# One-row matmul replaced by a ScalarE add, and a 64-row product widened to 128 rows, in an attention and two-MLP kernel

## The chip, the cores and the metric

The kernel runs on one core of a Trainium2 chip. The metric is the device time of one launch in microseconds. Three runs of the kernel before took 1377.99, 1380.79 and 1382.39 us, so the median is 1380.79 us. Five engines work side by side, each through its own queue in order: PE (TensorE), DVE (VectorE), ACT (ScalarE), POOL (GpSimd) and SP, which issues the DMAs.

## The reference

Attention over 4 batches, 8 heads, 576 positions and 64 channels, in which each row keeps only its 32 largest scores, then two MLPs (512 to 2048 to 512) over the 2304 tokens.

```
scores = scale * q @ k.T
kth    = 32nd largest of each row
p      = exp(where(scores >= kth, scores, -1e9) - max)
x      = p / (sum(p) + 1e-9) @ v
x      = softplus-like(x @ w_in) @ w_out           # first MLP
h      = x @ w_in2;  out = (h - tanh(h)) @ w_out2  # second MLP
```

The change is in the third and fourth lines: the product of p and v, and the 1e-9 in the divisor.

## The kernel before, in words

Every float32 operand is split into two float16 halves (high and low), and a product is made of three: high by high, high by low and low by high.

A tile is 128 queries of one head (kind "n", 128 tiles), or 64 left-over queries of each of two heads (kind "l", 16 tiles); there are 144. Its steps lie on all engines. `front` makes the scores on PE (L554), and ACT copies them out of PSUM (L557). `chain` finds the 32nd largest on DVE, with four MAX8 and three MATCH_REPLACE8 over 576 columns (L566, L569). `exps` and `mask` make p on ACT (L134). `turn` casts p to its halves (ACT L596, POOL L597 and L598) and transposes them by DMA into `pT`, of two buffers. `back` multiplies `pT` by the values and normalizes. Its result goes by another DMA transpose into x, the first MLP's input.

In `back`, a head's product is a run of matmuls of 65 columns: 64 channels and a column of ones in `vh`, which gives the sum of p. The 576 keys are four blocks of 128 and one of 64 (SL). For a full block t there are L612, L613 and L614. In the last block, partitions 0 to 63 of `pT[:, NB]` hold the high half of p, and 64 to 127 its low half; the values of that block stand twice in `vh` and `vl`, on both halves of the partitions. L615 is over all 128 rows: high by high and low by high at once. L616 is high p by low v, over 64 rows. L618 multiplies a row of ones (1 partition, float32) by eps and adds it into the sum's column; a float32 matmul shows as two records. DVE then takes the reciprocal straight from PSUM (L629), POOL multiplies it by a factor for kind "l" alone (L631), ACT scales the 64 channels out of PSUM (L636). A tile of kind "n" has one such run of matmuls ("side"), one of kind "l" two: 160 in all.

PSUM has four buffers "tp", which `back` (px), the MLPs' first product (h) and small column sums (pn) share.

An MLP step is 24 matmuls of 256 columns (h: L680 to L682), an activation (ACT L134, L701, POOL L702, L705, for the second MLP also DVE L699), and, three or four steps later, 24 matmuls of 256 columns (L723 to L725) or 12 of 512 (L731 to L733). The program emits steps for about one tile's worth of tokens with each tile as soon as the weights of that MLP have been split. The splitting (L277 to L316, all engines) fills the early part. A scheduler then orders each engine's queue by priorities and its own estimates.

Of the kernel before, what the change touches and what calls it, by code (L numbers as in the profile page):

```python
# [13 lines left out]
AF = mybir.ActivationFunctionType  # L14
# [59 lines left out]
def topk_attention_two_mlps(  # L74
# [17 lines left out]
    nc = tc.nc  # L92
    P = 128
    B, H, S, D = q.shape
# [3 lines left out]
    NB = 4  # L98
    SL = S - NB * P
# [45 lines left out]
    def tiny(n=1):  # L145
        o = used_[0]
        used_[0] += n
        return tiles_[:, o : o + n]

    ones = tiny()  # L150
# [3 lines left out]
    eps = tiny()  # L154
    nc.gpsimd.memset(eps, 1e-9)
    eps2 = tiny()
# [4 lines left out]
    def nm(s):  # L161
        uid[0] += 1
        return f"{s}_{uid[0]}"
# [438 lines left out]
    def back(st):  # L602
        vi, it = st.vi, st.it
        ps = ps_t.tile([P, 512], F32, tag="tp", name=nm("px"))
        if st.kind == "n":
            sides = [(ps[:, 0 : D + 1], st.h, 0, P)]
        else:
            sides = [(ps[0:SL, j * (D + 1) : (j + 1) * (D + 1)], j, j * SL, (j + 1) * SL) for j in range(2)]
        for o, h, c0, c1 in sides:
            vh, vl = vi.vhl[:, 0, h], vi.vhl[:, 1, h]  # L610
            for t in range(NB):
                nc.tensor.matmul(o, st.pT[:, t, c0:c1], vh[:, t, 0 : D + 1], start=(t == 0), stop=False)  # L612
                nc.tensor.matmul(o, st.pT[:, t, c0:c1], vl[:, t, 0 : D + 1], start=False, stop=False)  # L613
                nc.tensor.matmul(o, st.pT[:, NB + 1 + t, c0:c1], vh[:, t, 0 : D + 1], start=False, stop=False)  # L614
            nc.tensor.matmul(o, st.pT[:, NB, c0:c1], vh[:, NB, 0 : D + 1], start=False, stop=False)  # L615
            nc.tensor.matmul(o, st.pT[0:SL, NB, c0:c1], vl[0:SL, NB, 0 : D + 1], start=False, stop=False)  # L616

            nc.tensor.matmul(o[:, D : D + 1], ones[0:1].to_broadcast([1, c1 - c0]), (eps2 if st.soft else eps)[0:1], start=False, stop=True)  # L618
        if st is it.sts[0]:
            it.x = ap.tile([P, 2, P], F16, tag="xs", bufs=NXS, name=nm("xs"))  # L620
            if XE:
                it.x32 = ap.tile([P, P], F32, tag="x32", bufs=NXS, name=nm("x32"))
        rows = P if st.kind == "n" else SL
        ns = len(sides)
        r = sp.tile([P, 2], F32, tag="r2", bufs=3, name=nm("r2"))

        pv = ps[0:rows, 0 : ns * (D + 1)].rearrange("p (j d) -> p j d", j=ns)
        rr = r[0:rows, 0:ns].unsqueeze(2)
        nc.vector.reciprocal(rr, pv[:, :, D : D + 1])  # L629
        if st.kind == "l":  # L630
            nc.gpsimd.tensor_mul(r[0:rows, 0:ns], r[0:rows, 0:ns], fl[vi.b][0:rows].to_broadcast([rows, ns]))  # L631
        for i, (o, h, c0, c1) in enumerate(sides):
            c = slice(h * D, (h + 1) * D)
            sc, src = r[0:rows, i : i + 1], o[:, 0:D]
            if XE:
                nc.scalar.activation(it.x32[0:rows, c], src, AF.Copy, scale=sc)  # L636
            else:
                nc.scalar.activation(it.x[0:rows, 0, c], src, AF.Copy, scale=sc)
                nc.vector.scalar_tensor_tensor(it.x[0:rows, 1, c], src, sc, it.x[0:rows, 0, c], op0=ALU.mult, op1=ALU.subtract)
        if st is not it.sts[-1]:  # L640
            return
        if XE:
            if XE == 1:
                nc.scalar.copy(it.x[0:rows, 0, :], it.x32[0:rows])
            else:
                nc.vector.tensor_copy(it.x[0:rows, 0, :], it.x32[0:rows])
            nc.gpsimd.tensor_sub(it.x[0:rows, 1, :], it.x32[0:rows], it.x[0:rows, 0, :])
        nc.sync.dma_start_transpose(
            out=it.chunk.x.block(vi.p)[:, :, it.col : it.col + rows],
            in_=it.x[0:rows].rearrange("p r c -> p (r c)"),  # L650
        )
# [203 lines left out]
    for ch, ts, _ in plan:  # L855
        for p in range(NP):
# [9 lines left out]
            for h in range(2):  # L866
                for ti, it in enumerate(its):
                    st = ST()
# [3 lines left out]
                if h == 0 and lc is not None:  # L872
                    it = ST()
                    it.spec, it.chunk, it.col, it.sts = vspec, lc, (ch.b % 2) * SL, []
                    st = ST()
# [71 lines left out]
    c1 = [0]  # L947
# [65 lines left out]
    for n in range(-1, NT + 2 + BL):  # L1013
# [12 lines left out]
        if last is not None:  # L1026
            ch = last.it.chunk
            if not hasattr(ch, "x"):
                while ch.T // P > len(xy_free):
                    force_step(n - 2 - BL)  # L1030
                ch.x = new_xy(ch.T, "x")
            with tc.high_priority(HP):
                back(last)
        if n + 1 < NT and n + 1 >= 0:
            st = tiles[n + 1]
# [74 lines left out]
```

## Time and profile before

| | us |
|---|---|
| median of three runs | 1380.79 |
| the profiled execution | 1381.37 |
| its span, first to last instruction | 1379.6 |
| PE busy | 1137.5 (82%) |
| DVE busy | 994.6 (72%) |
| ACT busy | 951.4 (69%) |
| POOL busy | 841.0 (61%) |

The busy shares are means over stages that differ. Up to about 414 us PE is busy half of the time or less, while the weights are split; from there to 1242 us tiles and MLP steps run together; after 1242 us only MLP steps are left. The stages have to be read one by one. The profiled execution is 1.8 us longer than its span.

### The profile page before, as it was taken

How to read it: one execution, taken by the hardware profiler on the slowest of the kernel's cores; microseconds unless marked ns; L12 is line 12 of the kernel's file. 1: busy time of each engine (PE TensorE's matmuls, PEld its weight loads, DVE VectorE, ACT ScalarE, POOL GpSimd, SP SyncE). 2: the span in 40 equal slices, each digit the busy share in tenths (PEclk: the TensorE clock that was granted, in tenths of full speed). 3: DMA queues.
4: the chain of work that ended last, by engine and by line, in shares of the span. 5: the costliest groups of instructions: out<-in, count | busy, mean ns of one | idle time of the engine just before them, and what ended most of it. 6: DMA issues, size and time to landing. Idle time of an engine off the chain costs nothing.

```text
span 1379.6 us, 28066 instructions
## 1 busy us (share of the span) xinstructions
PE 1137.5 (82%) x10098; PEld 882.1 (64%) x10098; DVE 994.6 (72%) x2150; ACT 951.4 (69%) x1786; POOL 841.0 (61%) x1194
## 2 busy tenths in 40 slices
PE   2232437975479999998999999999999899999998
PEld 1131225864358766767667987687767677896875
DVE  5998879979997697865878679759977688611011
ACT  7987988889886787655666767667764667643332
POOL 2679867887874665644666556557764366543342
PEclk9999998985568999989899999999999799999999
DMA  8956786565666458334456335435543254110000
GB/s 263 277 169 176 205 225 165 110 138 132 159 150 167 102 120 153 64 83 95 91 107 129 74 68 94 90 93 119 119 95 75 45 101 92 28 26 1 17 9 16
DMA packets 322524, 153.18 MB, mean 111 GB/s; under 512 B 270160, under 2 KB 302416, under 8 KB 322384
## 3 DMA queue, kind: packets, MB, share of 16 engines
q1 hardware_dynamic: 322384, 151.39, 47.8%
q8 instruction: 79, 1.29, 0.4%
q14 instruction: 61, 0.50, 0.1%
HBM read 73.04 MB, written 15.37 MB: 64 GB/s over the span
## 4 chain that ended last, share of the span: by engine, by line
PE 55%; DMA 11%; POOL 10%; DVE 9%; ACT 8%; issue 7%; SPq 1%; POOLq 0%; ACTq 0%
PE h L680 8%; PE h L681 8%; PE h L682 8%; DMA pT<-hl 4%; PE y L733 4%; PE y L731 4%; PE y L732 4%; PE s L554 3%; PE y L723 3%; PE y L724 3%; PE y L725 3%; DVE m L566 3%; DVE x L569 2%; PE px L618 2%; POOL wlo L316 2%
## 5 line engine op out<-in xcount | busy, mean ns | idle before, releaser
L566 DVE MAX8 m<-x 128x8 f32<-128x576 f32 x432 | 318.9, 749 | 3.5
L702 POOL TENSOR_SCALAR r<-r,gs 128x512 f32<-128x512 f32 (+1 forms) x160 | 109.1, 682 | 200.3 <-ACT g L701 175.6
L597 POOL TENSOR_TENSOR hl<-x,hl 128x512 f16<-128x512 f32 x144 | 170.4, 1183 | 90.6 <-ACT hl L596 76.7
L569 DVE MATCH_REPLACE8 x<-m,x 128x576 f32<-128x576 f32 x288 | 213.2, 741 | 0.0
L554 PE MATMUL s<-kT,qT 128*128 128x288 f16 x512 | 118.8, 324 | 82.6 <-ACT ssb L557 48.4
L705 POOL TENSOR_TENSOR g<-r,g 128x512 f16<-128x512 f32 (+1 forms) x160 | 172.4, 1078 | 9.4
L134 ACT ACTIVATE r<-h,hin 128x512 f32<-128x512 f32 (+1 forms) x160 | 102.1, 639 | 110.1 <-PE h L682 93.9
L680 PE MATMUL h<-y,whi 128*128 128x256 f16 (+1 forms) x640 | 166.0, 269 | 8.5 <-ACT y L751 8.5
L699 DVE SCALAR_TENSOR_TENSOR r<-h,hin,r 128x512 f32<-128x512 f32 (+1 forms) x80 | 55.1, 690 | 159.5 <-ACT r L134 153.1
L680 PE MATMUL h<-x,whi 128*128 128x256 f16 (+1 forms) x640 | 167.7, 270 | 0.7 <-DMA x<-xs 0.7
L682 PE MATMUL h<-x,wlo 128*128 128x256 f16 (+1 forms) x640 | 167.5, 270 | 0.0
L681 PE MATMUL h<-x,whi 128*128 128x256 f16 (+1 forms) x640 | 167.5, 270 | 0.0
L724 PE MATMUL y<-g,whi 128*128 128x256 f16 (+1 forms) x640 | 164.5, 267 | 2.1 <-POOL g L705 2.1
L681 PE MATMUL h<-y,whi 128*128 128x256 f16 (+1 forms) x640 | 166.0, 268 | 0.0
L682 PE MATMUL h<-y,wlo 128*128 128x256 f16 (+1 forms) x640 | 165.5, 268 | 0.0
L723 PE MATMUL y<-g,whi 128*128 128x256 f16 (+1 forms) x640 | 163.9, 268 | 1.0 <-ACT g L701 0.5
L725 PE MATMUL y<-g,wlo 128*128 128x256 f16 (+1 forms) x640 | 164.4, 267 | 0.0
L701 ACT ACTIVATE g<-r,gs 128x512 f16<-128x512 f32 (+1 forms) x160 | 107.6, 674 | 73.6 <-PE y L724 36.5
L566 DVE MAX8 m<-ssb 128x8 f32<-128x576 f32 x144 | 107.9, 749 | 60.3 <-ACT ssb L557 60.0
L612 PE MATMUL px<-vhl,pT 128*128 128x65 f16 (+1 forms) x640 | 97.5, 209 | 63.0 <-DMA pT<-hl 60.7
L680 PEld LDWEIGHTS <-whi 128*128 128x128 f16 x1280 | 128.2, 100 | 21.6
L681 PEld LDWEIGHTS <-whi 128*128 128x128 f16 x1280 | 127.9, 100 | 19.9 <-issue 1.0
(141 smaller groups left out, 3246.6 us busy)
## 6 DMA issues: line engine op xcount, KB each, us to landing
whi<-in_moe_w_in_dram SPq DMA_DIRECT2D x8, 1024.0 KB, 5.6
wlo<-in_moe_w_in_dram SPq DMA_DIRECT2D x6, 1024.0 KB, 7.5
wlo<-in_moe_w_out_dram SPq DMA_DIRECT2D x6, 1024.0 KB, 5.1
vd<-vhl SPq DMA_DIRECT2D x16, 330.0 KB, 3.2
vhl<-vd SPq DMA_DIRECT2D x16, 330.0 KB, 3.5
kd<-kT SPq DMA_DIRECT2D x32, 160.0 KB, 2.0
whi<-in_moe_w_out_dram SPq DMA_DIRECT2D x5, 1024.0 KB, 4.9
kT<-kd SPq DMA_DIRECT2D x32, 160.0 KB, 2.5
```

The lines of the kernel that those rows point to most:

```text
L554: nc.tensor.matmul(ps[:, hf, 0:HS], lhs, rhs[:, hf * HS : (hf + 1) * HS], start=(i == 0), stop=(i == len(prods) - 1))
L566: return lambda: nc.vector.max(m[:, 8 * i : 8 * i + 8], src)
L569: return lambda: nc.vector.match_replace(x, m[:, 8 * i : 8 * i + 8], src, NEG)
L597: nc.gpsimd.tensor_sub(hl[:, S + SL : 2 * S], st.p[:, 0 : NB * P], hl[:, 0 : NB * P])
L680: nc.tensor.matmul(o, hi[:, f], xhi, start=(d == 0), stop=False)
L681: nc.tensor.matmul(o, hi[:, f], xlo, start=False, stop=False)
L682: nc.tensor.matmul(o, lo[:, f], xhi, start=False, stop=(d == ND - 1))
L702: nc.gpsimd.tensor_scalar(r, r, gs, 1.0, op0=ALU.mult, op1=ALU.mult)
L705: nc.gpsimd.tensor_sub(glo, r, ghi)
L723: nc.tensor.matmul(o, hi[:, dd], gh, start=first, stop=False)
L724: nc.tensor.matmul(o, hi[:, dd], gl, start=False, stop=False)
L725: nc.tensor.matmul(o, lo[:, dd], gh, start=False, stop=fin)
```

## The change

L616 and L618 go. L617 takes L616's place, over all 128 rows: the upper 64 rows add the low half of p by the low half of v, a term that was left out so far. ACT adds eps to the sum on its way from PSUM to the small tile r (L628), with eps as a bias of one number per partition, and DVE takes the reciprocal of r in place (L629).

```
-            nc.tensor.matmul(o, st.pT[0:SL, NB, c0:c1], vl[0:SL, NB, 0 : D + 1], start=False, stop=False)
-
-            nc.tensor.matmul(o[:, D : D + 1], ones[0:1].to_broadcast([1, c1 - c0]), (eps2 if st.soft else eps)[0:1], start=False, stop=True)
+
+            nc.tensor.matmul(o, st.pT[:, NB, c0:c1], vl[:, NB, 0 : D + 1], start=False, stop=True)
...
-        nc.vector.reciprocal(rr, pv[:, :, D : D + 1])
+        nc.scalar.activation(rr, pv[:, :, D : D + 1], AF.Identity, bias=(eps2 if st.soft else eps)[0:rows])
+        nc.vector.reciprocal(r[0:rows, 0:ns], r[0:rows, 0:ns])
```

PE loses 160 instructions of L618 and swaps 160 pairs of load and matmul of L616 for L617's; ACT gains 144 instructions; DVE, POOL and SP keep their counts. The scheduler makes the queues anew. The three places below belong to one tile, whose product runs at about 702 us in the trace of before. PE, the end of the tile's product (px is its PSUM buffer, h that of an MLP step), before and then after:

```order
L614 MATMUL px_8291<-vhl_7703,pT_8174 128x65
L615 LDWEIGHTS pT_8174
L615 MATMUL px_8291<-vhl_7703,pT_8174 128x65
L616 LDWEIGHTS pT_8174
L616 MATMUL px_8291<-vhl_7703,pT_8174 128x65
L618 MATMUL px_8291<-tiny 128x1
L681 LDWEIGHTS whi_93
L681 MATMUL h_8227<-y_7488,whi_93 128x256
```

```order
L614 MATMUL px_8283<-vhl_7695,pT_8166 128x65
L615 LDWEIGHTS pT_8166
L615 MATMUL px_8283<-vhl_7695,pT_8166 128x65
L617 LDWEIGHTS pT_8166
L617 MATMUL px_8283<-vhl_7695,pT_8166 128x65
L681 LDWEIGHTS whi_93
L681 MATMUL h_8219<-y_7481,whi_93 128x256
```

The product ends with L617, and the MLP's L681 follows it as it followed L618; nothing else moved here.

ACT at the same tile (khl and vhl are halves of a later tile's keys and values, g an MLP step's), before and then after:

```order
L557 COPY ssb_8318<-s_8313 128x576
L701 ACTIVATE g_8138<-r_8137,gs_7507 128x512
L477 ACTIVATE khl_8617<-kraw_8094,tiny 128x5x64
L532 ACTIVATE vhl_8511<-v_7694,tiny 128x10x64
L636 ACTIVATE x_1441_8083<-px_8291,r_1481_8307 128x64
```

```order
L557 COPY ssb_8310<-s_8305 128x576
L477 ACTIVATE khl_8609<-kraw_8086,tiny 128x5x64
L701 ACTIVATE g_8130<-r_8129,gs_7500 128x512
L628 ACTIVATE r_1481_8298<-px_8283,tiny 128x1
L532 ACTIVATE vhl_8503<-v_7686,tiny 128x10x64
L636 ACTIVATE x_1441_8074<-px_8283,r_1481_8298 128x64
```

L628 stands behind L477 and L701, whose order has changed, and one instruction ahead of L636.

DVE at the same tile (m and x are those of a later tile's chain), before and then after:

```order
L566 MAX m_8373<-ssb_8318 128x8
L566 MAX m_8281<-x_8282 128x8
L569 MATCH_REPLACE x_8374<-m_8373,ssb_8318 128x576
L629 RECIPROCAL r_1481_8307<-px_8291 128x1
L566 MAX m_8373<-x_8374 128x8
L533 SCALAR_TENSOR_TENSOR vhl_8511<-v_7694,tiny,vhl_8511 128x10x64
```

```order
L569 MATCH_REPLACE x_8366<-m_8365,ssb_8310 128x576
L566 MAX m_8273<-x_8274 128x8
L629 RECIPROCAL r_1481_8298<-r_1481_8298 128x1
L566 MAX m_8365<-x_8366 128x8
L533 SCALAR_TENSOR_TENSOR vhl_8503<-v_7686,tiny,vhl_8503 128x10x64
```

The reciprocal has kept its place between the same steps of the chain, but it now reads what ACT wrote.

## Rows read from the trace of the kernel before

**Rows 1.** Busy us (instructions) by engine, clock, DMA, in three stretches.

```profile
0.00:414.00 414.00, 205.72 (x1566) 163.42 (x1567) 357.77 (x794) 351.27 (x675) 309.05 (x393) 0.86 0.69 181
414.00:1242.00 828.00, 799.18 (x7451) 621.00 (x7450) 622.04 (x1331) 555.56 (x1042) 483.22 (x741) 0.95 0.45 93
1242.00:1380.00 138.00, 132.60 (x1085) 97.71 (x1082) 14.76 (x27) 44.54 (x70) 48.77 (x61) 0.99 0.03 11
```

**Rows 2.** The chain that ended last, 414 to 1242 us, by line.

```profile
by line: PE h L681 10.2%; PE h L680 10.2%; PE h L682 10.0%; PE s L554 5.2%; PE y L733 4.4%; PE y L731 4.3%; PE y L732 4.3%; PE y L723 4.3%; PE y L724 4.2%; PE y L725 4.2%; issue 3.8%; PE px L618 3.3%; DMA pT<-hl 3.0%; PE px L612 2.2%; DMA v
```

**Rows 3.** PE in order of time: start us, us, instruction; a product's end.

```profile
702.20 0.19 PE L614 MATMUL px<-vhl,pT 128*128 128x65 f16 x1
702.22 0.20 PE L615 MATMUL px<-vhl,pT 128*128 128x65 f16 x1
702.35 0.20 PE L616 MATMUL px<-vhl,pT 64*128 64x65 f16 x1
702.48 0.38 PE L618 MATMUL px<-tiny 1*128 1x1 f32 x2
702.79 0.28 PE L681 MATMUL h<-y,whi 128*128 128x256 f16 x1
702.91 0.27 PE L682 MATMUL h<-y,wlo 128*128 128x256 f16 x1
```

**Rows 4.** PE in order of time, an end interleaved with an MLP step.

```profile
619.96 0.19 PE L615 MATMUL px<-vhl,pT 128*128 128x65 f16 x1
619.99 0.27 PE L681 MATMUL h<-x,whi 128*128 128x256 f16 x1
620.19 0.20 PE L616 MATMUL px<-vhl,pT 64*128 64x65 f16 x1
620.33 0.28 PE L682 MATMUL h<-x,wlo 128*128 128x256 f16 x1
620.54 0.38 PE L618 MATMUL px<-tiny 1*128 1x1 f32 x2
620.85 0.28 PE L680 MATMUL h<-x,whi 128*128 128x256 f16 x1
```

**Rows 5.** L618 alone in the first two stretches: PE busy (records), load busy, clock, DMA.

```profile
0.00:414.00 414.00, 22.12 (x88) 18.38 (x88) 0.86 0.69 181
414.00:1242.00 828.00, 42.77 (x232) 32.88 (x232) 0.95 0.45 93
```

**Rows 6.** L629 alone in the same stretches: DVE busy (instructions).

```profile
0.00:414.00 414.00, 6.27 (x40) 0.86 0.69 181
414.00:1242.00 828.00, 16.30 (x104) 0.95 0.45 93
```

**Rows 7.** Groups by line and shape: busy us, mean ns, idle before.

```profile
L636 ACT ACTIVATE x<-px,r 128x64 f32<-128x64 f32 x128 | 39.4, 308 | 42.2 <-DVE r L629 40.7 <-DVE tiny L180 1.4
L343 ACT ACTIVATION_READ_ACCUMULATOR vst<-vst 128x1 f32 x60 | 11.3, 189 | 0.0
L510 ACT ACTIVATE ql<-ql,tiny 128x64 f32<-128x64 f32 x16 | 5.5, 344 | 4.8 <-DMA ql<-in_q_dram 3.8 <-POOL hl L598 0.8 <-DVE tiny L179 0.2
```

**Rows 8.** Waits, 0 to 414 us: us in total, times, longest.

```profile
PE px L612 <- DMA pT<-hl: 54.7, 20, 13.0
PE pn L169 <- ACT wlo L288: 51.1, 19, 8.0
PE s L554 <- ACT ssb L557: 43.5, 19, 7.8
```

**Rows 9.** Waits, 414 to 1242 us.

```profile
DVE r L629 <- PE px L618: 46.0, 27, 6.7
ACT x L636 <- DVE r L629: 36.4, 26, 3.7
PE h L680 <- ACT y L751: 8.5, 2, 4.4
```

**Rows 10.** ACT and DVE in order of time, near 707 us.

```profile
707.31 0.56 ACT L477 ACTIVATE khl<-kraw,tiny 128x320 f16<-128x320 f32 x1 [2.29 <-DMA kT<-khl]
706.90 0.16 DVE L629 RECIPROCAL r<-px 128x1 f32<-128x1 f32 x1
```

**Rows 11.** Busy by engine and clock, two slices around the change of stage.

```profile
345.00:414.00 69.00, 41.33 (x316) 31.96 (x317) 65.55 (x158) 57.23 (x126) 55.56 (x95) 0.60 0.65 154
414.00:483.00 69.00, 64.75 (x606) 55.35 (x605) 49.94 (x124) 49.14 (x103) 37.66 (x56) 0.94 0.59 135
```

## The prediction

> **What bounds the kernel now.** I read the busy time by stretch first, since the change touches PE and ACT and the page's means mix three stages. The reader is to see three kernels in one [rows 1]. Up to 414 us PE works 205.7 us of 414, while DVE (357.8) and ACT (351.3) are both at 85 to 86%: no engine is full, and work passes from one to the next. From 414 to 1242 us PE is busy 799 of 828 us, 97%, at a granted clock of 0.95, with DVE at 75% and ACT at 67%: PE bounds this stage. After 1242 us PE is alone at 96%, and no product of p and v is left there, as L618 has no record [rows 5].
>
> A busy PE may still hide slack, so I read the chain of waits of the middle stage next [rows 2]. Its largest shares are PE's: the listed lines of h, y, s and px add up to 67%. L618 alone, a matmul of one column, holds 3.3% of it. Then I read PE in order of time at the end of a product, for the spacing of starts, since ends are modelled and overlap [rows 3, 4]. Then the waits, for who would be late if PE were early [rows 8, 9].
>
> **PE: what goes.** In the plain form [rows 3] L615 starts at 702.22 and the next step's L681 at 702.79: the end of the product holds PE for 0.57 us. Without L616 and L618 it holds L615 and L617, two 128-row matmuls of 65 columns. Such a one hands over after 0.03 us (L615 to L681) [rows 4], so 0.06 us stay and 0.51 go. In the interleaved form [rows 4] L615 to L680 takes 0.89 us and holds two matmuls of h, worth 0.12 each by the spacing in rows 3; 0.65 are the product's, 0.06 stay, 0.59 go. Where the time goes shows in the same rows: 0.13 us pass before L616 starts where 0.03 is usual, 0.13 more before L618, and 0.31 from L618 to the next matmul.
>
> The Trainium skill ("TensorEngine Tiling (Array Packing)", Key Properties) says that changing the tiling mode drains TensorE. By that rule the 0.13 us ahead of L616 belong to its 64 rows and fall to 0.03 with L617. Without it, they may belong to the end of the product and stay. The rows agree with the rule at one place each, but show no 128-row matmul in L616's position.
>
> How many: the middle stage has 232 records of L618, two each, so 116 sides [rows 5]. At 0.51 to 0.59 us this is 59 to 68 us of PE. I take 0.53, near the plain form, which is the commoner in the stretches I read: 62 us.
>
> How much of that arrives: L618 lies in the chain with 3.3% of 828 us = 27 us [rows 2]. All its 116 sides would be 116 x 0.31 = 36 us. So about 0.76 of them stand where time is made; the others stand where the chain runs over a transpose, DVE or ACT. 62 x 0.76 = 47 us. The ends are 0 (PE only waits longer) and the full 68.
>
> In the first stage 44 sides go as well, at 0.5 us or more each, 22 us of PE or more. PE is half idle there and waits for transposes, for ACT's sums and for its evictions of scores, 149 us in the three longest of its waits [rows 8]. I count this gain as nothing; the idle time covers it. If it did arrive, it would be up to 22.
>
> **ACT: what comes.** 144 instructions L628 of 128x1, from PSUM, with a bias per partition. The trace has none. From below: 189 ns, a read of 128x1 without operands (L343) [rows 7]. From above: 344 ns, 64 columns with a per-partition operand (L510) [rows 7]; L636, from PSUM with 64 columns, takes 308. I take 250, between the ends, since one column is left of 64: 36 us in all, 27 to 50 by the ends.
>
> The 104 tiles of the middle stage [rows 6] bring 26 us, which lift ACT from 556 of 828 to 582 of about 781 us, 75%: hidden beside PE, which runs three to four MLP steps ahead of the activations it waits for. If this cover fails, all 26 are paid. The 40 tiles of the first stage bring 10 us on an engine at 85% in a stage without a full engine. I charge half, 5 us; the ends are a gain of 5 (a shorter PE part in the same chain) and a loss of 25, below.
>
> **DVE: what moves.** The reciprocals stay 144 and read one column of SBUF in place of PSUM. I cost this at nothing: the row of before is 16.30 us for 104, 157 ns each [rows 6], and cannot fall by more. What matters is the wait. DVE waited 46 us for PE at L629 in the middle stage [rows 9], and ACT then 36 us for DVE at L636. Now ACT waits for PE, DVE for ACT, and ACT again for DVE. PE's part comes 0.5 us earlier, L628 and its handover cost about 0.3, so the reciprocal is ready at about the same time if ACT is there. If ACT is not, DVE's next MAX8 stands behind the reciprocal, as the order shows. The scheduler left five or fewer instructions of ACT between L628 and L636 at 112 of 144 tiles, fourteen at most.
>
> Nothing else moves: the number of DMAs and their queue are the same, and by the order the MLP steps stand at the same tiles as before, within a few matmuls. The longer hold of a PSUM buffer px (one more hop, under 1 us) meets four buffers, and no wait of PE for one of them is among the long ones.
>
> **The sum.** 1381.4 (profiled) - 47 + 5 = 1339. The median of the runs lies 0.6 us lower than the profiled execution, inside the rounding: I forecast **1339 us**, with a range of its own of 1318 to 1360 (a share of 0.95 or 0.45 of the 62 us arriving, with the 5 of the first stage).
>
> **Rivals.**
>
> *DVE gets stuck behind ACT (slower).* At 707 us ACT waits 2.29 us for a transpose at L477 until 707.31, then works 0.56 us; DVE's reciprocal starts at 706.90 [rows 10]. In the new order L628 is behind this L477: it would end at about 708.1, and DVE would wait 1.2 us where it waited for nothing. If that is the usual case, the first stage has 40 x 1.2 = 48 us of new waits on an engine with 56 us to spare; charge 40. In the middle stage 104 x 1.2 = 125 us bring DVE from 622 to 747 of 781 us, and half of PE's 47 us is lost. 1381 + 40 - 23 = 1398. It decides once the mean new wait is over 1 us a tile. Against it: DVE already waited for px at 27 of 104 tiles in the middle stage, and the order puts other work between.
>
> *The spacing stays.* If the 0.13 us ahead of the last two matmuls belong to the product's end, 0.57 falls to 0.13 + 0.13 only, and 0.31 a side goes: 116 x 0.31 x 0.76 = 27 us; 1381 - 27 + 5 = 1359.
>
> *Hidden.* PE finishes earlier and waits longer for what the others bring, one for one: 1381, within 4. For it speaks that a third of the chain is not PE's; against it that all of PE's waits for another engine in the middle stage are short, the longest in total 8.5 us [rows 9].
>
> *The clock.* From 345 to 414 us the granted clock is 0.60, the 1.2 GHz level most of the time, with PE busy 41 of 69 us; in the next slice it is 0.94 with 65 [rows 11]. If a sparser PE stayed low for one slice more, that slice's 64.75 us of work would take 64.75 x 0.94 / 0.60 = 101, 37 more: 1376. The Trainium skill ("TensorE: Matmul & The Clock Gate", HAM oscillation) states that pauses between bursts of matmuls throw the clock back to half. The trace agrees in that the low slice is the one with pauses. Against this rival: little PE work leaves one slice, about 3 us of 65.
>
> *All of it.* The full 68 us arrive, and the first stage loses nothing: 1313.
>
> **Chances.** Forecast 0.60; spacing stays 0.08; clock 0.04; all of it 0.10; hidden 0.07; DVE behind ACT 0.11. A change under 0.3% (4 us) can't be told from none here. Faster: 0.60 + 0.08 + 0.04 + 0.10 = 0.82, with the clock's case just on its edge; same 0.07; slower 0.11. The range leaves out the last two and goes down to the full gain less a little for the first stage: 1308 to 1376.
>
> **What would show it.** Right: no spacing over 0.05 us inside the product's end, L617 to the next matmul too; PE's busy share after 414 us near 97% still, in a stage shorter by some 45 us; attention's end at about 1200 in place of 1242 us, the tail after it unchanged; the first 40 tiles done within 5 us of 414; L628 at 0.25 us. Wrong: DVE's wait at L629 for ACT over 100 us in all, or PE's waits in the middle stage grown by 30 us or more, or a spacing of 0.13 us ahead of L617.

## The result and the profile after

The changed kernel takes 1329.05 us (median of 4 runs, 1323.64 to 1331.66) where the kernel before took 1381.59 beside it: a ratio of 0.962, 95% interval 0.958 to 0.965. Forecast were 1339 us, in a range of 1308 to 1376. The profiled execution took 1329.11 us with a span of 1327.1.

The view of busy time by engine in the kernel after, in the three stretches of [rows 1] with the middle one cut where attention now ends; the columns are those of [rows 1]:

```profile
0.00:414.00 414.00, 178.44 (x1457) 141.42 (x1458) 356.95 (x780) 353.03 (x707) 298.48 (x383) 0.82 0.69 180
414.00:1190.00 776.00, 729.32 (x7242) 571.90 (x7241) 624.44 (x1345) 572.18 (x1155) 487.23 (x752) 0.97 0.49 100
1190.00:1327.10 137.10, 132.47 (x1083) 97.61 (x1081) 14.62 (x27) 44.56 (x70) 48.74 (x61) 0.99 0.03 11
```

PE is at 94% in the middle stage, where it was at 97%; DVE rose from 75 to 80%, ACT from 67 to 74%. The last stretch is as it was. To see which stage gave the time, both traces are cut where a tile number is the same: at the 41st reciprocal and at the last one (the 144th). Before:

```profile
0.00:420.50 420.50, 212.22 (x1628) 169.05 (x1629) 364.03 (x807) 356.11 (x687) 313.55 (x398) 0.86 0.69 180
420.50:1220.20 799.70, 770.88 (x7138) 596.13 (x7136) 611.47 (x1309) 541.68 (x1014) 470.84 (x723) 0.95 0.46 95
1220.20:1379.60 159.40, 154.40 (x1336) 116.94 (x1334) 19.07 (x36) 53.57 (x85) 56.64 (x73) 0.99 0.03 10
```

After:

```profile
0.00:431.30 431.30, 192.66 (x1606) 154.02 (x1606) 374.22 (x821) 367.75 (x740) 311.75 (x403) 0.83 0.68 178
431.30:1168.60 737.30, 693.70 (x6851) 540.48 (x6849) 602.71 (x1294) 548.54 (x1105) 466.17 (x718) 0.97 0.50 101
1168.60:1327.10 158.50, 153.87 (x1328) 116.42 (x1325) 19.08 (x36) 53.48 (x85) 56.53 (x73) 0.99 0.03 10
```

The first stage became 10.8 us longer, the middle one 62.4 us shorter, the last 0.9 shorter: 52.5 in all. In the middle PE's busy time fell by 77 us and its idle time rose from 28.8 to 43.6. The granted clock rose there from 0.95 to 0.97. Length times granted clock is the length that the stage would have at 2.4 GHz: 799.7 x 0.95 = 760 and 737.3 x 0.97 = 715, 45 us less. The other 17 us are then what the 1.2 GHz level cost before and no longer costs: the stage spends some 35 us less at that level, at half the clock. (The clock has two digits, so each product is good to some 4 us, and the reckoning takes the whole stage to run at PE's pace.) By the same reckoning PE's busy time fell by 59 us: 770.88 x 0.95 = 732, 693.70 x 0.97 = 673.

PE in order of time at the end of a product, the answer to [rows 3]:

```profile
655.14 0.19 PE L614 MATMUL px<-vhl,pT 128*128 128x65 f16 x1
655.17 0.19 PE L615 MATMUL px<-vhl,pT 128*128 128x65 f16 x1
655.21 0.19 PE L617 MATMUL px<-vhl,pT 128*128 128x65 f16 x1
655.23 0.27 PE L680 MATMUL h<-y,whi 128*128 128x256 f16 x1
```

From L615 to the MLP's next matmul there are 0.06 us, where there were 0.57. The chain of waits from 414 to 1190 us, by line, the answer to [rows 2]:

```profile
by line: PE h L681 7.0%; PE h L680 7.0%; PE h L682 7.0%; DMA pT<-hl 6.8%; issue 6.7%; DVE m L566 4.6%; DVE x L569 4.2%; PE y L724 3.7%; PE y L723 3.7%; PE y L725 3.6%; PE s L554 3.4%; POOL hl L597 2.5%; PE y L731 2.5%; PE y L732 2.4%; PE y 
```

PE's shares are smaller, and the transpose of p, DVE's MAX8 and MATCH_REPLACE8 stand among them now: the next bounds are near. The small instructions by line and shape (busy us, mean ns, idle before), and the waits from 414 to 1190 us, the answer to [rows 7, 9]:

```profile
L628 ACT ACTIVATE r<-px,tiny 128x1 f32<-128x1 f32 x128 | 32.9, 259 | 20.2 <-PE px L617 19.6
L629 DVE RECIPROCAL r<-r 128x1 f32<-128x1 f32 x128 | 18.9, 149 | 14.1 <-ACT r L628 13.8
```

```profile
DVE r L629 <- ACT r L628: 26.4, 15, 5.4
ACT x L636 <- DVE r L629: 22.7, 23, 2.6
ACT r L628 <- PE px L617: 21.3, 20, 2.5
PE px L612 <- DMA pT<-hl: 20.9, 20, 2.1
PE h L680 <- ACT y L751: 9.8, 2, 5.4
```

L628 takes 259 ns. DVE's wait at the reciprocal has fallen from 46.0 us, for PE (38.1 of them up to 1190 us), to 26.4, for ACT; PE waits 20.9 us for the transposes of p, where it waited 5.8 in the same stretch before. In the first stage PE's same three waits grew from 149 us [rows 8] to 182:

```profile
PE pn L169 <- ACT wlo L288: 72.3, 18, 12.5
PE s L554 <- ACT ssb L557: 57.9, 22, 8.8
PE px L612 <- DMA pT<-hl: 52.3, 16, 9.7
```

The granted clock of the first stage can't be read from the column in these views. The view of the kernel after by stretch, for L612 alone (PE busy, load busy, clock, DMA):

```profile
0.00:188.00 188.00, 7.94 (x44) 6.41 (x44) 1.00 0.80 227
192.00:232.00 40.00, 4.39 (x24) 3.02 (x24) 0.50 0.63 149
407.00:440.00 33.00, 1.98 (x16) 1.57 (x16) 1.00 0.65 160
```

The view by source of the same line in the same stretches gives the time of one of its matmuls, all of one shape (ns: least, median, most):

```profile
L612 PE MATMUL px<-vhl,pT x44: 215/243/262, 62.3 to 186.2; 128*128 128x65 f16 x44
L612 PE MATMUL px<-vhl,pT x24: 233/243/247, 194.7 to 227.8; 128*128 128x65 f16 x24
L612 PE MATMUL px<-vhl,pT x16: 190/194/204, 411.5 to 432.1; 128*128 128x65 f16 x16
```

Up to 188 us the column shows 1.00, but the matmul takes the 243 ns that it takes at 0.50, and not 194. In the kernel before it takes 243 ns up to 207 us as well, with 1.00 in the column. So the clock is compared in the middle stage alone.

### The profile page after: what moved, and what is told of

Its sections match the earlier page's. It is cut to its first block, busy times and chain, and to the rows that moved or that the text cites. A ratio compares the mean times of both kernels' runs of the same rounds, so it can differ in the third digit from the quotient of the medians.

```text
span 1327.1 us, 27583 instructions
## 1 busy us (share of the span) xinstructions
PE 1040.2 (78%) x9778; PEld 810.9 (61%) x9778; DVE 996.0 (75%) x2150; ACT 969.8 (73%) x1930; POOL 834.4 (63%) x1194
## 4 chain that ended last, share of the span: by engine, by line
PE 40%; DVE 15%; DMA 13%; POOL 12%; ACT 10%; issue 9%; SPq 1%; POOLq 0%; ACTq 0%; DVEq 0%
PE h L680 6%; PE h L681 6%; PE h L682 6%; DVE m L566 5%; DMA pT<-hl 5%; DVE x L569 5%; PE y L724 3%; PE y L723 3%; PE y L731 3%; PE y L725 3%; PE y L732 3%; PE y L733 3%; POOL hl L597 3%; PE s L554 2%; POOL wlo L316 2%
## 5 line engine op out<-in xcount | busy, mean ns | idle before, releaser
L680 PE MATMUL h<-y,whi 128*128 128x256 f16 (+1 forms) x640 | 162.7, 263 | 10.2 <-ACT y L751 9.8
L681 PE MATMUL h<-x,whi 128*128 128x256 f16 (+1 forms) x640 | 166.7, 269 | 0.0
L681 PE MATMUL h<-y,whi 128*128 128x256 f16 (+1 forms) x640 | 162.4, 263 | 0.0
L682 PE MATMUL h<-y,wlo 128*128 128x256 f16 (+1 forms) x640 | 162.3, 263 | 0.0
L612 PE MATMUL px<-vhl,pT 128*128 128x65 f16 (+1 forms) x640 | 96.3, 209 | 79.6 <-DMA pT<-hl 73.3
L701 ACT ACTIVATE g<-r,gs 128x512 f16<-128x512 f32 (+1 forms) x160 | 107.8, 676 | 57.0 <-PE y L724 25.0
L681 PEld LDWEIGHTS <-whi 128*128 128x128 f16 x1280 | 126.6, 99 | 22.5 <-issue 4.3
```

The source lines that it names most:

```text
L680: nc.tensor.matmul(o, hi[:, f], xhi, start=(d == 0), stop=False)
L681: nc.tensor.matmul(o, hi[:, f], xlo, start=False, stop=False)
L682: nc.tensor.matmul(o, lo[:, f], xhi, start=False, stop=(d == ND - 1))
```

## The experiments

The theory was that PE's time at the end of each product is the price ("PE"). The rivals were that the hop over ScalarE matters, for or against, and that the gain is in how the scheduler's queues fall. All times are medians, beside runs of the kernel before on the same chip (1377.01 in the first group, 1378.55 and 1378.54 in the others); the ratio stands behind, with its 95% interval. The changed kernel's 1329.05 was taken beside 1381.59, so a difference between it and a form below is good to a few us.

**The wide product alone**

```
-  nc.tensor.matmul(o, st.pT[0:SL, NB, c0:c1], vl[0:SL, NB, 0 : D + 1], start=False, stop=False)
+  nc.tensor.matmul(o, st.pT[:, NB, c0:c1], vl[:, NB, 0 : D + 1], start=False, stop=False)
```

> The wide product alone (L617 over 128 rows); the one-row matmul for 1e-9 stays. Theory PE (the end of each product holds PE, and the spacing ahead of a matmul of other rows is the price): only the 0.10 us ahead of the 64-row matmul goes, the one-row matmul still has 0.13 ahead of it and 0.31 behind, so 116 x 0.10 = 12 us of PE go and 9 to 12 arrive: 1370 to 1373 us. Theory 'spacing belongs to the product's end': nothing goes, 1381. Theory 'new order' (the gain is in how the queues fall, not in PE's time): anything, up to the whole 52 us, 1329.

Measured: 1367.67 us, 0.993 (0.990 to 0.996). The scheduler gave every engine the same queue as in the kernel before, so nothing but PE's spacing differs. PE in order of time:

```profile
697.89 0.19 PE L615 MATMUL px<-vhl,pT 128*128 128x65 f16 x1
697.92 0.19 PE L616 MATMUL px<-vhl,pT 128*128 128x65 f16 x1
698.05 0.38 PE L618 MATMUL px<-tiny 1*128 1x1 f32 x2
698.36 0.28 PE L681 MATMUL h<-y,whi 128*128 128x256 f16 x1
```

The 0.13 us ahead of the last product are 0.03 now, those ahead of the one-row matmul have stayed. 116 x 0.10 = 12 us of PE went and 9 arrived, as expected of theory PE. "Spacing belongs to the product's end" is out. What differs in the spacing shows in the weight loads (PEld), in the kernel before and then here:

```profile
702.20 0.10 PEld L615 LDWEIGHTS <-pT 128*128 128x128 f16 x1
702.35 0.09 PEld L616 LDWEIGHTS <-pT 64*128 64x128 f16 x1
```

```profile
697.86 0.10 PEld L615 LDWEIGHTS <-pT 128*128 128x128 f16 x1
697.89 0.10 PEld L616 LDWEIGHTS <-pT 128*128 128x128 f16 x1
```

Over 128 rows the load of L616 starts with the matmul before it (697.89), 0.03 us ahead of its own; over 64 rows it starts only with its own matmul, 0.13 us behind L615's start.

**The add on ScalarE alone** (the changed kernel with the last product over 64 rows)

```
-  nc.tensor.matmul(o, st.pT[:, NB, c0:c1], vl[:, NB, 0 : D + 1], start=False, stop=True)
+  nc.tensor.matmul(o, st.pT[0:SL, NB, c0:c1], vl[0:SL, NB, 0 : D + 1], start=False, stop=True)
```

> The add on ScalarE alone; the last product stays over 64 rows and is now the last matmul. Theory PE: 0.13 us ahead of L616 stays and about 0.13 behind it, of 0.57 us a side 0.29 stay and 0.28 go: 116 x 0.28 = 32 us, of which 0.8 to 0.9 arrive, less some 3 us for ScalarE: 1354 to 1360 us. Theory 'ScalarE's hop costs': under half of that arrives, 1365 or more. Theory 'new order': anything, 1329 too.

Measured: 1338.47 us, 0.972 (0.969 to 0.975), faster than any figure of theory PE, and with the queues of the changed kernel. This part of the change alone gives 38.5 us; the wide product gives 9 on top, as it does alone. (The two make 48 of the 52.5; the other 4.6 is the distance between the two medians of the kernel before.) The middle stage, from the 41st to the last reciprocal:

```profile
427.70:1175.60 747.90, 718.98 (x6853) 554.58 (x6851) 603.43 (x1295) 550.02 (x1105) 467.65 (x718) 0.96 0.48 100
```

Length times clock is 718 here, 42 us under the kernel before, and PE's busy time at 2.4 GHz (690) fell by 42 as well: all of it arrived, within the two digits. From here to the changed kernel, with the same queues, PE's busy time falls by another 25 us, but its idle time rises from 28.9 to 43.6, and length times clock goes from 718 to 715 only.

**The wide product without 1e-9, and the 64-row product without it**

```
-  nc.scalar.activation(rr, pv[:, :, D : D + 1], AF.Identity, bias=...)
-  nc.vector.reciprocal(r[0:rows, 0:ns], r[0:rows, 0:ns])
+  nc.vector.reciprocal(rr, pv[:, :, D : D + 1])
```

These are the lines of the first form, against the changed kernel. The second has, besides, L617 over 64 rows as in "The add on ScalarE alone".

> The wide product, and 1e-9 is added nowhere (left out): VectorE takes the reciprocal straight from PSUM. Against the changed kernel it takes away 144 ScalarE instructions (37 us busy) and one hop between the product and the reciprocal. Theory PE (ScalarE's part is covered): 1320 to 1328 us. Theory 'the hop costs': the waits of VectorE for ScalarE (26 us) and the first stage's 10 us come back, 1305 or less.

> The last product over 64 rows, and 1e-9 is added nowhere (left out). Theory PE: like the add alone without ScalarE's cost, 1350 to 1357 us, and 25 to 32 us over the wide product without 1e-9; each of the 64-row matmul's two spacings of 0.13 us is to be seen in the order of time. Theory 'spacing belongs to the product's end': the same time as the wide product without 1e-9.

Measured: 1352.7 us, 0.982 (0.978 to 0.986), and 1364.04 us, 0.991 (0.987 to 0.994). A miss for every theory: with less work than the changed kernel the wide form is 24 us slower. The two have the same queues as each other, other ones than the rest, and differ by 11 us, where 25 to 32 were expected. The 64-row form in order of time:

```profile
696.57 0.19 PE L615 MATMUL px<-vhl,pT 128*128 128x65 f16 x1
696.70 0.20 PE L617 MATMUL px<-vhl,pT 64*128 64x65 f16 x1
696.83 0.28 PE L680 MATMUL h<-y,whi 128*128 128x256 f16 x1
```

A 64-row matmul between others costs 0.13 us ahead of it and 0.13 behind. The wide form in stages, to the 41st and to the last reciprocal:

```profile
0.00:441.20 441.20, 192.06 (x1576) 151.33 (x1577) 374.41 (x822) 360.87 (x694) 310.48 (x403) 0.87 0.66 173
441.20:1189.10 747.90, 701.55 (x6874) 545.39 (x6873) 602.89 (x1295) 535.09 (x1007) 467.53 (x719) 0.96 0.49 100
```

Against the changed kernel's profiled execution it loses 10 us before the 41st tile and 11 in the middle. There 747.9 x 0.96 = 718 us at 2.4 GHz are what the changed kernel has (715): the middle's 11 us are mostly clock, as far as its two digits tell.

**ScalarE's add to a tile that nobody reads**

```
-  nc.scalar.activation(rr, pv[:, :, D : D + 1], AF.Identity, bias=...)
-  nc.vector.reciprocal(r[0:rows, 0:ns], r[0:rows, 0:ns])
+  ru = sp.tile([P, 2], F32, tag="ru", bufs=3, name=nm("ru"))
+  nc.scalar.activation(ru[0:rows, 0:ns].unsqueeze(2), pv[:, :, D : D + 1], AF.Identity, bias=...)
+  nc.vector.reciprocal(rr, pv[:, :, D : D + 1])
```

> The changed kernel, but ScalarE's add goes to a tile that nobody reads, and VectorE takes the reciprocal straight from PSUM, without 1e-9 (left out of the result). Seen so far: without 1e-9 and without the add 1353 us, with the add 1329. Theory 'the hop helps' (VectorE's queue no longer waits on PE itself): the hop is gone, so about 1350 to 1358, as without the add. Theory 'order of the first stage' (the middle stage, tile 41 to the last reciprocal, takes 52 to 62 us less than before in all wide forms without the one-row matmul, and what differs between them is up to 25 us in how the queues fall before tile 41): middle stage 738 to 750 us in place of 800, and a total between 1325 and 1358 that goes with tile 41's time. Theory 'ScalarE's time costs' (37 us busy): slower than without the add, 1360.

Measured: 1343.69 us, 0.976 (0.973 to 0.978), between the two. ScalarE's 37 us more did not make it slower than the form without an add. The middle stage:

```profile
427.80:1185.50 757.70, 709.97 (x6898) 550.81 (x6896) 604.07 (x1295) 553.17 (x1113) 467.24 (x721) 0.95 0.48 100
```

It is longer than the 738 to 750 us expected, and the 41st tile is 3.5 us earlier than the changed kernel's, though the total is 15 us longer. So "order of the first stage" falls too: the forms differ in the middle stage as well, here for the most part by clock (757.7 x 0.95 = 720).

**The add twice on ScalarE**

```
   nc.scalar.activation(rr, pv[:, :, D : D + 1], AF.Identity, bias=...)
+  nc.scalar.activation(rr, rr, AF.Identity, bias=...)
```

> The changed kernel with a second add of 1e-9 on ScalarE behind the first (the result has 2e-9 in the divisor). One more ScalarE instruction of some 0.25 us in the hop of each tile, 36 us busy in all. Theory PE (ScalarE is covered): middle stage 740 to 750 us, total within 8 us of the changed kernel unless the first stage's order differs. Theory 'the hop helps': not slower than the changed kernel, 1320 to 1332. Theory 'ScalarE's time costs': 0.25 us at each of 144 tiles, 1350 or more.

Measured: 1342.63 us, 0.975 (0.972 to 0.978). In stages:

```profile
0.00:439.40 439.40, 192.14 (x1584) 151.93 (x1585) 378.45 (x831) 375.37 (x783) 312.13 (x406) 0.87 0.66 176
439.40:1182.00 742.60, 699.00 (x6875) 545.47 (x6873) 598.74 (x1285) 567.05 (x1207) 461.34 (x717) 0.96 0.48 100
```

742.6 x 0.96 = 713 us: at 2.4 GHz the second add costs the middle stage nothing that can be seen, though ACT works 18.5 us more there and the queues are others. The first stage is 8 us longer than the changed kernel's, the total 14, outside the 8 us of theory PE.

**The add on VectorE**

```
-  nc.scalar.activation(rr, pv[:, :, D : D + 1], AF.Identity, bias=...)
+  nc.vector.tensor_scalar(rr, pv[:, :, D : D + 1], (eps2 if st.soft else eps)[0:rows], None, op0=ALU.add)
```

> The add of 1e-9 on VectorE, from PSUM, ahead of its reciprocal; ScalarE has no part in it. VectorE waits on PE itself, as without the add, and has 144 instructions of some 0.15 us more. Theory 'the hop helps': as slow as without 1e-9 or slower, 1350 to 1362. Theory 'order of the first stage': middle stage 740 to 752 us, total between 1328 and 1362 by tile 41's time.

Measured: 1333.33 us, 0.969 (0.965 to 0.972), 1325.81 to 1344.5 over its runs. VectorE waits on PE itself here and is as fast as the changed kernel within its spread. So "the hop helps" falls. In stages, from the profiled execution, the fastest of the six:

```profile
0.00:429.80 429.80, 192.28 (x1586) 152.57 (x1587) 375.76 (x853) 358.24 (x692) 308.61 (x399) 0.87 0.69 177
429.80:1165.60 735.80, 690.56 (x6872) 542.39 (x6870) 616.40 (x1407) 535.73 (x1009) 466.75 (x723) 0.97 0.50 102
```

**The matmul for 1e-9 over 128 rows** (with the wide product)

```
-  nc.tensor.matmul(o[:, D : D + 1], ones[0:1].to_broadcast([1, c1 - c0]), (eps2 if st.soft else eps)[0:1], ...)
+  nc.tensor.matmul(o[:, D : D + 1], ones.to_broadcast([P, c1 - c0]), (eps2 if st.soft else eps), ...)
```

> The wide product, and the matmul for 1e-9 kept, but over 128 rows of ones in place of one (it adds 128 times 1e-9). Theory 'change of rows' (the spacing ahead of a matmul whose number of rows differs): the 0.12 us ahead of L618 falls to about 0.03 and some of the 0.18 us behind it goes; 0.46 us a side becomes 0.25 to 0.35: 13 to 24 us under the wide product alone, 1345 to 1356. Theory 'float32 matmul': the spacing is that of its two passes and weight loads and stays: 1368.

Measured: 1352.67 us, 0.982 (0.979 to 0.985), with the queues of the kernel before. PE in order of time:

```profile
697.01 0.20 PE L615 MATMUL px<-vhl,pT 128*128 128x65 f16 x1
697.05 0.19 PE L616 MATMUL px<-vhl,pT 128*128 128x65 f16 x1
697.08 0.36 PE L618 MATMUL px<-tiny 128*128 128x1 f32 x2
697.30 0.27 PE L681 MATMUL h<-y,whi 128*128 128x256 f16 x1
```

The float32 matmul of 128 rows has 0.03 us ahead of it and 0.22 until the next start, 0.25 in all, where the one of one row had 0.13 and 0.31, 0.44. So 0.19 of the one-row matmul's 0.44 us was the change of rows; 15 us come back without any engine but PE being touched, inside the 13 to 24 of "change of rows". The middle stage:

```profile
418.40:1191.60 773.20, 732.55 (x7113) 572.49 (x7112) 608.72 (x1310) 539.92 (x1013) 470.68 (x723) 0.95 0.47 98
```

**Other orders of the same instructions** (both kernels with HP, one number of the scheduler's priorities, at 48 and 52)

```
-HP = 50
+HP = 48
```

The second form of each has 52 in place of 48.

> The kernel before with one number of the scheduler's priorities changed (HP 48 in place of 50): the same instructions in another order. The five forms whose products end alike (L617's 128 rows, no one-row matmul) came out between 1329 and 1353 us. Theory 'order luck' (an order is worth up to 12 us either way whatever it computes): 1367 to 1391, with the middle stage at about 800 us and differences mainly before tile 41. Theory 'no luck' (the differences among the five come from where the add sits): 1379 within 4.

> The kernel before with HP 52: another order of the same instructions. 'Order luck': 1367 to 1391; 'no luck': 1379 within 4. With HP 48 and the kernel before itself it gives a mean over three orders.

> The changed kernel with HP 48: another order of the same instructions. 'Order luck' (the five wide forms have a mean of 1340, the changed kernel drew one of the best orders): 1330 to 1350, more likely slower than 1329 than faster. 'No luck': 1329 within 4.

> The changed kernel with HP 52: another order of the same instructions. 'Order luck': 1330 to 1350; 'no luck': 1329 within 4. If PE's shorter ends are worth what the orders kept fixed show, the mean of three orders of the changed kernel lies about 40 us under that of three orders of the kernel before.

Measured: the kernel before 1382.4 us, 1.003 (1.001 to 1.005), and 1374.22, 0.998 (0.996 to 1.000); the changed kernel 1336.56, 0.971 (0.968 to 0.974), and 1331.93, 0.967 (0.965 to 0.970). Three orders each: before 1374 to 1382, mean 1378; after 1329 to 1337, mean 1333. The change is worth 46 us over three orders, and an order is worth some 4 us either way here. That is less than the 12 of "order luck" and, for the changed kernel with HP 48, more than the 4 of "no luck"; it does not reach the 24 us by which the form without 1e-9 is slower. The middle stage of the four, in the order of the texts above:

```profile
420.60:1222.80 802.20, 774.55 (x7124) 590.62 (x7122) 613.22 (x1309) 541.79 (x1013) 467.43 (x723) 0.95 0.45 95
424.60:1212.50 787.90, 761.81 (x7122) 590.01 (x7121) 611.27 (x1310) 539.26 (x1010) 472.43 (x725) 0.96 0.47 96
438.30:1184.60 746.30, 698.31 (x6865) 542.77 (x6864) 602.74 (x1294) 545.43 (x1105) 464.06 (x718) 0.97 0.48 100
431.10:1167.00 735.90, 693.70 (x6866) 541.74 (x6865) 602.46 (x1294) 546.51 (x1105) 466.05 (x718) 0.97 0.50 102
```

With the orders of HP 50, the middle stage is on the mean 57 us shorter after the change and 42 by length times clock (760, 762 and 756 before; 715, 724 and 714 after), and the 41st tile comes on the mean 12 us later.

## Why the prediction was right, point by point

**The size of a product's end** was right: 0.57 us before and 0.06 after. The two spacings of 0.13 us went. The Trainium skill ("TensorEngine Tiling (Array Packing)", Key Properties) says that a change of tiling mode drains TensorE. The runs agree in where the time is lost: 0.13 us ahead of a matmul of other rows, 0.03 ahead of one of the same. They show the late weight load; whether a drain holds it back they don't show.

**How much of it arrives** was right by the measure that leaves the clock out. Forecast were 62 us, of which 0.76, or 47, arrive. At 2.4 GHz the middle stage became 45 us shorter, and 59 us of PE's busy time went. With the queues of before and L618 wide the stage takes 773.2 us at 0.95, 735 at 2.4 GHz against 760, so 25 us of 116 x 0.28 = 32 arrive. But the share is not the same for each part: of the 42 us of the add alone all arrive, and of what the wide product takes off after that hardly any (718 to 715). So 0.76 fits the whole change, to the few us that two digits and an order leave; that the lines of one matmul in the chain give the share of every part is not shown. All seven profiles of forms whose product ends in L617 alone have 713 to 724 us there, by the same product of length and clock.

**The clock** was named as a rival against the change, with the wrong sign for the middle stage: 0.95 became 0.97, some 17 us. That is more than the 15 by which the stage beats its forecast (62 against 47). All three orders show it: 0.95, 0.95 and 0.96 before, 0.97 in each after. It does not follow from the amount of PE's work alone: the wide form without 1e-9 and those with an unread add and with two adds have the same products on PE and 0.96, 0.95 and 0.96. What sets it there is not known. For the first stage the sign can't be told, since its column shows 1.00 where a matmul takes as long as at 0.50.

**The first stage** was mis-sized: +5 forecast, +10.8 measured, 17.7 and 6.5 with HP 48 and 52. The forecast's sign of being right, the first 40 tiles within 5 us, failed with it. Its cause is not settled. All forms without the matmul for 1e-9 reach their 41st tile at 428 to 446 us, with or without ScalarE's add; those that keep it, at 418 to 425. ScalarE's add can't be the whole of it, since the form without any add is at 441. A second add went with 8 us more there, but in another order. What the missing matmul does to the queues of the weights' splitting is not known.

**ScalarE's add** was right in price (0.25 us forecast, 0.26 measured) and, within some 4 us, in its cover in the middle stage: the doubled add, in queues of its own, has 713 us at 2.4 GHz there against 715.

**The hidden gain and the stuck VectorE** did not come. PE's idle time in the middle stage rose by 15 us, a share of the gain that was given back; 30 were the sign of being wrong. So PE's busy share is 94% there and not near 97%, as the forecast had it. VectorE's wait at L629 for ScalarE is 26 us, a quarter of a microsecond a tile of the middle stage, where 1 us would have decided.

**The number** is nearer than its terms. The middle stage gave 15 us more than forecast and the first stage took 6 more; the tail gave 1. The total came out 10 us under the forecast, and the part that the clock gave was luck: nothing in the sum stands for it. With the 45 us of PE alone and the first stage as measured it would be 1381 - 45 + 11 = 1347, 8 over the forecast. The ends of the range of its own, 1318 and 1360, take the first stage's 5 us once as a gain and once as a loss; the upper one comes to 1381.4 - 27.9 + 5 = 1358.5.

What stays open is the 24 us between the changed kernel and the form without 1e-9 (21 in the profiled executions): about half before the 41st tile and the other half mostly clock. The two other orders of the changed kernel are 3 and 8 us slower than it, so an order of that kind isn't worth as much; why that form's queues are worse is not known.

## What to carry to other kernels

In an accumulation whose matmuls all have 128 rows, one with 64 rows cost 0.1 us more on either side here; padding it to 128 rows with data that adds nothing harmful was cheaper, and the float32 constant was better added outside. How much of a removed line stands in the chain of waits is a first guess for how much of a saving on a bounding engine arrives; expect less of the last part, where PE's idle time grows as it did here. Look at the granted clock before calling the rest a surprise, and check a clock of 1.00 against the time of one matmul of a fixed shape. Where a scheduler remakes the queues, compare forms that keep the same queues first, and give each kernel two or three orders before a difference of one per cent is explained.

## What the runs showed of the hardware that was not expected

Between two forms with the same products on PE the middle stage's length moved more with the granted clock than with all else: the wide form with an unread add has 0.95 there and 757.7 us, that with the add on VectorE 0.97 and 735.8, but 720 and 714 us at 2.4 GHz. Over 64 rows a weight load started 0.13 us behind the matmul before it, over 128 rows together with it. Up to 188 us of the kernel after the clock's column shows 1.00 while a 128x65 matmul takes 243 ns, as at 0.50, and not 194. In the kernel with two adds, an ACTIVATE of one column from PSUM with a bias per partition took 258 ns (median), the second, in place in SBUF, 294.
